# One kernel, one queue: SyncE's DMA instructions in program order through the whole attention stage

## The chip, the core and the metric

The kernel runs on one core of a Trainium2 chip. The metric is the device time of one execution in microseconds. In the profile TensorE is PE (its weight loads PEld), VectorE is DVE, ScalarE is ACT, GpSimd is POOL and SyncE is SP. SP computes nothing here: it is the queue from which most DMAs are issued, and its instructions appear as SPq. An instruction that has to wait holds up everything behind it on its own engine's queue. POOL issues DMAs too: the gathers and scatters by index, and the loads that convert their data on the way.

## What is computed

Block-causal attention over 8 batches and 8 heads, and on its rows a mixture of experts with one expert for each row:

```python
scores = scale * np.matmul(q, k.transpose(0, 1, 3, 2))          # q, k, v: (8, 8, 576, 64) float32
scores = np.where(block_i >= block_j, scores, -1e9)              # blocks of 64 positions
attn = softmax(scores); attn_out = np.matmul(attn, v)            # (8, 8, 576, 64)
x = attn_out.transpose(0, 2, 1, 3).reshape(8 * 576, 512)         # 4608 rows
logits = x @ w_gate + modality_bias[modality_id]                 # 8 experts
e_idx = argmax(logits); gate_w = softmax(logits)[e_idx]
out[rows of e] = gate_w * (relu(x[rows of e] @ w1[e]) @ w2[e])   # 512 -> 1024 -> 512
```

Everything is kept to float32 precision: PE's operands are split into a high and a low part, and each product is summed from several matmuls.

## The kernel before

**Attention** works on pairs of heads: 32 pairs, four pairs to a batch. A loop over slots (`run_slot`) works on pair `slot` and on pair `slot - 1` at once, by a list of steps written out by hand (`ORDER`; `FIRST` for slot 0, `LAST` for slot 32): scores S, maxima M, exponentials E, transposes T, their copies C and rests D, the products with v in the parts X, Y and W, the copies x and y, the product K with the gate's weights and an identity, and the rows Z. Before its steps a slot issues the loads of later pairs: `load(slot + 2)` (the tile `raw`, the keys), `load_v(slot + 1)` (`vrt`) and `split_qk(slot + 1)`. The last makes the high and low parts of the next pair on POOL and issues three kinds of DMA on SP: two copies `k2t<-z`, one copy `z<-qkt`, and the load `rawq` (queries) of the pair after. PE's first scores of a slot (L259, L260, step SA2) read that slot's `z`.

**Routing.** When the last pair of a batch b has its rows in the tile `xr` (and the 64 late positions in `xt`), `routing(b)` returns a list of some twenty small steps, which are taken one by one where `ORDER` has a q. One of them is `weight_out` (L503 to L514): two reciprocals on DVE (L504, L505), and then on SP the write of `xr` into the DRAM rows `xrows` (L507), two writes of `xt` (L511), the write of `wt` (L512) and a small load `idt` (L514), which the scatters into the expert lists will need. It falls near the end of slot 4b + 6, and for the last batches somewhat earlier.

**Into the experts.** During slots 30 to 32 the first expert's weights are loaded already (class `Experts`, `early`): `raw<-w` on SP (L809), a converted copy of each chunk on POOL (L813, called casts here), and the low part by a subtraction on POOL or DVE (L818). The row numbers of the first expert come by `ids_lead` (L831). Two gathers on POOL (L839, one for 128 rows) fetch 256 rows from `xrows` into `xr_124`, the tile that holds the rows of batch 6 until their write (L507) has read it. Their transposes (L852, step turn0) are PE's first work in slot 32, in front of the last pair's products (L383) and of the first expert product (L870). After attention `run_all` goes through parts of 256 rows, PE after PE product, to the end.

**What sets the order.** The kernel is written for a framework that orders instructions itself. Inside `manual_schedule(engines=...)` the named engines keep the order in which the program issues. PE, ACT, DVE and POOL are named all through. SP is named for the start and the first four slots:

Of the kernel before, what the change touches and what calls it, by code (L numbers as in the profile page):

```python
# [24 lines left out]
NPAIR = B * H // 2  # L25
# [11 lines left out]
LEAD = SLOT * NLEAD  # L37
BIG = float(1 << 20)
NWARM = 12
NSP = 4  # L40
SCALE = 0.125
GUARD = 1e-9
CHUNK_OFF = (0, 128, 384, 768)
# [49 lines left out]
def attention_moe(ctx, tc, qk, vr, bkw, mid, mb, w1, w2, cf, ci, cm, ld, out):  # L93
# [68 lines left out]
    def load(p):  # L162
        d = pairs[p]
        d.qk = qkts[p % 3]
        d.q = d.qk[:, 0:1280].rearrange("p (h c) -> p h c", h=2)
        d.k = d.qk[:, 1280:2432].rearrange("p (h c) -> p h c", h=2)
        d.qt = d.qk[:, 2432:2560]
        d.raw = raws[p % 2]
        d.q2, d.k2, d.pt = q2s[p % 2], k2s[p % 2], pts[p % 2]
        d.s, d.pm, d.copies, d.o, d.ot, d.b = {}, {}, {}, {}, {}, {}  # L170
        d.ott = None
        if p < 2:
            for h in range(2):
                ks, qs = halves(h)
                nc.sync.dma_start(d.raw[:, ks], qk[p][:, 1280:2560][:, ks])
                if p == 0:
                    nc.sync.dma_start(rawq[:, qs], qk[p][:, qs])
            pool.dma_start(zs[p][64:68], cm)
        else:
            nc.sync.dma_start(d.raw, qk[p][:, 1280:2560])  # L180
# [17 lines left out]
    def split_qk(p):  # L198
        d = pairs[p]
        k = d.raw[0:64, 0:1152].rearrange("p (h c) -> p h c", h=2)  # L200
        q = rawq[0:64].rearrange("p (h c) -> p h c", h=2)
        pool.tensor_copy(d.qk[:, 1280:2560], d.raw)
        pool.tensor_tensor(d.k2[0:64], k, d.k[0:64], ALU.subtract)  # L203
        gather_low(d)
        pool.tensor_copy(d.qk[:, 0:1280], rawq)
        nc.sync.dma_start(d.q2[0:64].bitcast(F32), d.q[64:128, :, 0:512].bitcast(F32))
        pool.tensor_tensor(d.q[0:64], q, d.q[0:64], ALU.subtract)  # L207
        load_q(p + 1)

    def split_half(p, h):  # L210
        d = pairs[p]
        ks, qs = halves(h)
        dve.tensor_copy(d.qk[:, 1280:2560][:, ks], d.raw[:, ks])
        act.copy(d.qk[:, qs], rawq[:, qs])
        (dve, pool)[p * h].tensor_tensor(d.k2[0:64, h], d.raw[0:64, 576 * h : 576 * h + 576], d.k[0:64, h], ALU.subtract)
        if h == 1:
            gather_low(d)
        act.copy(d.q2[0:64, h], rawq[0:64, qs][:, 0:512])
        (dve, pool)[p * h].tensor_tensor(d.q[0:64, h], rawq[0:64, qs], d.q[0:64, h], ALU.subtract)  # L219
        if (p, h) == (0, 1):  # L220
            load_q(1)
        if (p, h) == (1, 1):
            load(2)
            load_q(2)

    def load_v(p):
        d = pairs[p]
        d.vr = att.tile([128, 640], F32, name="vrt", bufs=3)
        nc.sync.dma_start(d.vr, vr[p])
        d.v = att.tile([128, 8, 2, 64], F32R, name="vhl", bufs=2)  # L230
# [337 lines left out]
    def choose(eng):  # L568
        lead, start = (cst.tile([128, NE], F32, name=n) for n in ("taken", "start"))
        eng.tensor_tensor(cnt, run, bases, ALU.subtract)  # L570
        sel["oha"], sel["ea"] = pick(eng, cnt, "a", kx, ranks)
        oha = sel["oha"]
        eng.scalar_tensor_tensor(cnb, oha, -BIG, cnt, ALU.mult, ALU.add)
        eng.scalar_tensor_tensor(lead, cnt, float(LEAD), oha, ALU.min, ALU.mult)
        sel["ohb"], sel["eb"] = pick(eng, cnb, "b", kx, ranks)
        eng.tensor_tensor(rest, lead, bases, ALU.add)
        sel["ra"] = dot(eng, oha, bases, "a")
        sel["rr"] = dot(eng, oha, rest, "r")
        sel["rb"] = dot(eng, sel["ohb"], bases, "b")
        eng.scalar_tensor_tensor(begin, oha, float(COVER - LEAD), rest, ALU.mult, ALU.add)  # L580
        eng.scalar_tensor_tensor(start, sel["ohb"], float(COVER_B), begin, ALU.mult, ALU.add)
        sel["start"] = start

    def emit(name, p):
        u = name[1:]
        if name == "vh":
            split_v(p)
        elif name == "r":
            sums(p)
        elif name == "p":  # L590
            inverses(p)
        elif name[0] == "S":
            scores(p, u)
        elif name[0] == "M":
            maxima(p, u)
        elif name[0] == "E":
            exps(p, u)
        elif name[0] == "T":
            transposes(p, u)
        elif name[0] == "C":  # L600
            copies(p, u)
        elif name[0] == "D":
            rests(p, u)
        elif name[0] in "XYW":
            values(p, "AB".index(u), name[0])
        elif name[0] in "xy":
            keep(p, "AB".index(u), name[0])
        elif name[0] == "K":
            back(p, "AB".index(u))
        elif name[0] == "Z":  # L610
            rows(p, "AB".index(u))

    done = set()
    lag = max(s for n, s in ORDER if n[0] != "q")
# [39 lines left out]
    def run_slot(slot):  # L654
        nonlocal steps, ex
        if 0 < slot < NPAIR - 2:
            load(slot + 2)
        if 0 < slot < NPAIR - 1:
            if slot > 1:
                load_v(slot + 1)  # L660
            split_qk(slot + 1)
        for name, stage in LAST if slot == NPAIR else ORDER if slot else FIRST:
            p = slot - stage
            for what in EARLY_STEPS.get((slot, name), ()):
                if ex is None:
                    ex = Experts(ctx, tc, cst, scratch, btmp, con["edges"], xrows, idlist, idf, w1, w2, out, sel, run, base8, pick, dot, ps_s, ps_t, ps_o, o0, placing, qkts, raws, zs, pts, xrb)
                ex.early(what)
            if name[0:6] == "+steps":
                for f in steps[0 : int(name[6:])]:
                    f()  # L670
                steps = steps[int(name[6:]) :]
                continue
            if name[0] == "+":
                ex.early(name[1:])
                continue
            if name[0] == "q":
                kind = "" if name[1].isdigit() else name
                for _ in range(2 if EARLY * PPB < slot < NPAIR - 1 and not kind else 1):
                    if slot > 1 and steps and getattr(steps[0], "kind", "") == kind:
                        steps.pop(0)()  # L680
                continue
            if not 0 <= p < NPAIR or (name, p) in done:
                continue
            assert slot < NPAIR or (name, 1) in ORDER
            if slot == 0:
                done.add((name, p))
                if name in first:
                    first[name]()
                    continue
            emit(name, p)  # L690
            if name == "vh":
                for _ in range(2):
                    if placing and slot < NPAIR:
                        g, c = placing.pop(0)
                        g(c)
            if name == "ZB" and p % PPB == PPB - 1:
                for f in steps:
                    f()
                steps = routing(p // PPB)
                if p // PPB == EARLY - 1:  # L700
                    choose(Later(dve, steps))

    engines = {ET.PE, ET.Activation, ET.DVE, ET.Pool}
    with tc.manual_schedule(engines=engines | {ET.SP}):
        load(0)
        for _ in range(NWARM):
            pe.matmul(bbank, ones, jks[0], start=True, stop=True)
        nc.sync.dma_start(cft, cf)
        split_half(0, 0)
        load(1)  # L710
        for slot in range(NSP):
            run_slot(slot)
    with tc.manual_schedule(engines=engines):
        for slot in range(NSP, NPAIR + lag):
            run_slot(slot)
        att_stack.close()
        ex.run_all(steps)
    ex.rest()
# [366 lines left out]
```

## Time and profile before

| | |
|---|---|
| median of 3 runs | 871.63 us (871.34 to 872.15) |
| the profiled execution | 871.13 us, of which the span from first to last instruction 869.5 us |
| mean granted TensorE clock | 0.983 |
| attention (slots 0 to 31) | up to about 408 us of the span |
| experts | from there to the end |

The rows that matter are quoted two sections down. In a timeline a row is one instruction or a run of like ones: its start, its duration, its engine and line, what it writes and reads, and in brackets how long its engine was idle before it and what ended that. For SP and POOL the duration of a DMA instruction is that of its issue; the data moves afterwards. A row of the windows gives for one stretch the busy time of each engine, PE's granted clock, the share of time in which the DMA engines were busy, and the rate.

### The profile page before, as it was taken

The page shows a single profiled execution, that of the slowest core. Times are in us where ns is not written, and L with a number is a line of the kernel's source. Part 1 is how long each engine was busy: PE and PEld are TensorE (multiplying, and loading weights), DVE is VectorE, ACT ScalarE, POOL GpSimd, SP SyncE. Part 2 cuts the span into 40 slices and gives each one's busy share as a digit, 9 for nine tenths or more (in the row PEclk, how much of TensorE's full clock was granted, in tenths as well). Part 3 has the DMA queues.
Part 4 walks back from the last instruction along what each step waited for, and adds up shares of the span by engine and source line. Part 5 has one row for each costly group of instructions (what it writes and reads, how often), then busy time and mean ns, then how long its engine had stood idle before and what let it go on. Part 6 is the DMA issues. An engine that isn't in the chain of part 4 may idle for free. (4 is left out here: it accounts for less than half of the span.)

```text
span 869.5 us, 16671 instructions
## 1 busy us (share of the span) xinstructions
PE 839.6 (97%) x5816; PEld 768.0 (88%) x5816; DVE 449.7 (52%) x1653; ACT 455.1 (52%) x1366; POOL 444.2 (51%) x300
## 2 busy tenths in 40 slices
PE   6999999999999999997999999999999999999995
PEld 4889999999999999897988999999999999999884
DVE  6798888888888888796442111111121122222120
ACT  6788888889888898786212222222222122222220
POOL 1967879798888979893864222222211111111100
PEclk8899999999999999999999999999999999999998
DMA  6869656766666667657752212212212222210100
GB/s 188 252 220 282 195 188 198 242 196 207 198 230 211 201 188 242 193 136 192 225 203 75 74 62 73 73 63 72 74 49 73 74 74 73 73 61 28 36 14 18
DMA packets 58183, 120.20 MB, mean 138 GB/s; under 512 B 13458, under 2 KB 24530, under 8 KB 58088
## 3 DMA queue, kind: packets, MB, share of 16 engines
q1 hardware_dynamic: 47344, 95.31, 35.7%
q0 software_dynamic: 10752, 23.79, 8.4%
q8 instruction: 48, 0.79, 0.4%
q14 instruction: 39, 0.32, 0.1%
HBM read 80.12 MB, written 22.25 MB: 118 GB/s over the span
## 5 line engine op out<-in xcount | busy, mean ns | idle before, releaser
L346 DVE TENSOR_TENSOR ptl<-t,pth 128x512 fp32r<-128x512 f32 (+3 forms) x288 | 139.9, 505 | 18.8 <-ACT pth L341 17.4
L341 ACT CAST pth<-t 128x512 fp32r<-128x512 f32 (+3 forms) x288 | 122.4, 452 | 36.2 <-PE t L316 22.8
L290 ACT ACTIVATE pm<-s,nm 128x256 f32<-128x256 f32 (+3 forms) x256 | 134.8, 535 | 11.3 <-DVE scratch L264 11.0
L264 DVE TENSOR_SCALAR_CACHE_REDUCE scratch<-s 128x128 bf16<-128x128 f32 (+4 forms) x288 | 133.0, 479 | 7.5 <-PE s L260 4.3
L383 PE MATMUL o<-pth,vhl 128*128 128x256 f32 (+1 forms) x384 | 116.2, 320 | 0.8 <-POOL vhl L236 0.6
L918 ACT ACTIVATE scratch<-o,gw 128x512 f32<-128x512 f32 x37 | 25.5, 689 | 173.0 <-PE o L916 102.0
L877 DVE SCALAR_TENSOR_TENSOR qkt<-s,qkt 128x512 fp32r<-128x512 f32 x18 | 12.4, 689 | 190.2 <-ACT qkt L876 190.2
L383 PE MATMUL o<-ptl,vhl 128*128 128x256 f32 (+1 forms) x384 | 109.3, 297 | 0.0
L203 POOL TENSOR_TENSOR z<-raw,qkt 64x1152 fp32r<-64x1152 f32 x30 | 79.5, 2650 | 47.7 <-issue 18.4
L919 POOL DMA_INDIRECT out<-scratch,ids_b x17 | 16.9, 996 | 162.7 <-ACT scratch L918 162.7
L259 PE MATMUL s<-qkt 128*128 128x256 f32 (+2 forms) x256 | 89.5, 360 | 3.7 <-DVE qkt L219 3.7
L870 PE MATMUL s<-z,w0hb 128*128 128x256 f32 x512 | 91.2, 281 | 0.0
L870 PE MATMUL s<-z,qkt 128*128 128x256 f32 x720 | 90.1, 283 | 0.6 <-issue 0.6
L870 PEld LDWEIGHTS s<-z,qkt 128*128 128x128 f32 x720 | 88.6, 192 | 1.3 <-issue 0.5
L207 POOL TENSOR_TENSOR qkt<-rawq,qkt 64x1280 fp32r<-64x1280 f32 x30 | 87.9, 2931 | 2.4
L260 PE MATMUL s<-z 68*128 68x256 f32 (+2 forms) x256 | 80.5, 330 | 0.0
L870 PEld LDWEIGHTS s<-z,w0hb 128*128 128x128 f32 x512 | 79.1, 188 | 0.6
L383 PEld LDWEIGHTS o<-pth,vhl 128*128 128x128 f32 x384 | 73.5, 191 | 3.1 <-POOL vhl L236 1.0
L383 PEld LDWEIGHTS o<-ptl,vhl 128*128 128x128 f32 x384 | 74.2, 193 | 1.4
L870 PE MATMUL s<-z,w0lb 128*128 128x256 f32 x256 | 71.9, 281 | 0.0
L402 PE MATMUL b<-bk,ot 128*128 128x72 f32 x512 | 64.7, 269 | 2.0 <-ACT pth L341 1.2
L402 PEld LDWEIGHTS b<-bk,ot 128*128 128x128 f32 x512 | 64.2, 192 | 2.4 <-ACT pth L341 1.4
(255 smaller groups left out, 1923.6 us busy)
## 6 DMA issues: line engine op xcount, KB each, us to landing
raw<-qk SPq DMA_DIRECT2D x30, 640.0 KB
rawq<-qk SPq DMA_DIRECT2D x30, 640.0 KB
raw<-w SPq DMA_DIRECT2D x23, 512.0 KB
vrt<-vr SPq DMA_DIRECT2D x32, 320.0 KB
k2t<-z SPq DMA_DIRECT2D x64, 144.0 KB
xrows<-xr SPq DMA_DIRECT2D x8, 1056.0 KB
z<-qkt SPq DMA_DIRECT2D x30, 256.0 KB
idlist<-btmp SPq DMA_DIRECT2D x8, 304.0 KB
```

Of the source, the lines that this page charges most:

```text
L203: pool.tensor_tensor(d.k2[0:64], k, d.k[0:64], ALU.subtract)
L207: pool.tensor_tensor(d.q[0:64], q, d.q[0:64], ALU.subtract)
L259: pe.matmul(o, d.q[:, h, qs], d.k[:, h, 0:n], start=True, stop=False)
L260: pe.matmul(o, d.q2[0:68, h, qs], d.k2[0:68, h, 0:n], start=False, stop=True)
L264: dve.tensor_scalar(jks[jturn[0] % 4][:, 0 : s.shape[-1]], s, -SCALE, start, ALU.mult, ALU.min, accum_out=o)
L290: act.activation(d.pm[h][:, CHUNK_OFF[c] : CHUNK_OFF[c] + n], s[:, 256 * i : 256 * i + n], AF.Exp, bias=d.nm[:, h, c : c + 1], scale=SCALE ...
L341: act.copy(dst[0], s)
L346: dve.tensor_tensor(dst[1], s, dst[0], ALU.subtract)
L383: pe.matmul(o, w, r, start=part != "W" and i == 0, stop=part != "Y" and i == len(mm) - 1)
L402: pe.matmul(d.b[h][:, 72 * c : 72 * c + 72], d.ot[h][:, 128 * c : 128 * c + 128], w, start=True, stop=True)
L870: nc.tensor.matmul(hp[:, a, :], w[:, kc, ms], x[:, kc, :], start=i == 0, stop=i == len(mm) - 1)
L918: nc.scalar.mul(yo, y, s.gw[:, i : i + 1])
```

## The change

The constant `NSP` goes, and the first of the two `manual_schedule` blocks, the one that names SP, takes all slots. The second block holds only what comes after attention.

```diff
-NSP = 4
...
         load(1)
-        for slot in range(NSP):
+        for slot in range(NPAIR + lag):
             run_slot(slot)
     with tc.manual_schedule(engines=engines):
-        for slot in range(NSP, NPAIR + lag):
-            run_slot(slot)
         att_stack.close()
         ex.run_all(steps)
```

Line numbers after the removed lines are lower by one to three (L507 becomes L506, L813 becomes L810). PE, DVE and ACT keep their instructions in the same order. The number of instructions is the same on every engine; SP's order changes, and POOL's in one place.

On SP around a batch's `weight_out`, here for batch 0 in slots 6 and 7, before. `z_111` takes the queries' second half of pair 7, `z_104` those of pair 8:

```order
L196 DMA k2t<-z_111 64x576 x2
L206 DMA z_111<-qkt_119 64x2x512
L188 DMA rawq<-qk 128x1280
L180 DMA raw_122<-qk 128x1280
L229 DMA vrt<-vr 128x640
L196 DMA k2t<-z_104 64x576 x2
L507 DMA xrows<-xr_124 128x4x528
L512 DMA xrows<-wt 64x16
L206 DMA z_104<-qkt_120 64x2x512
L188 DMA rawq<-qk 128x1280
```

And with the change:

```order
L195 DMA k2t<-z_111 64x576 x2
L205 DMA z_111<-qkt_119 64x2x512
L187 DMA rawq<-qk 128x1280
L506 DMA xrows<-xr_124 128x4x528
L510 DMA xrows<-xt 64x4x64 x2
L511 DMA xrows<-wt 64x16
L513 DMA idt<-ci 128x80
L179 DMA raw_122<-qk 128x1280
L228 DMA vrt<-vr 128x640
L195 DMA k2t<-z_104 64x576 x2
L205 DMA z_104<-qkt_120 64x2x512
L187 DMA rawq<-qk 128x1280
```

All five DMAs of `weight_out` now stand together between the load `rawq` of slot 6 and slot 7's loads; before, the two writes of `xt` went out a slot earlier, `idt` at some other time, and `xr` after the `k2t` copies of slot 7.

On SP in slot 30, before (`xr_124` holds batch 6, the `raw` loads are expert weights):

```order
L831 DMA ids_lead<-idlist 128x6x1
L809 ISA
L809 DMA raw_122<-w 128x4x256
L809 ISA
L809 DMA raw_121<-w 128x4x256
L507 DMA xrows<-xr_124 128x4x528
L512 DMA xrows<-wt 64x16
```

And with the change:

```order
L828 DMA ids_lead<-idlist 128x6x1
L506 DMA xrows<-xr_124 128x4x528
L510 DMA xrows<-xt 64x4x64 x2
L511 DMA xrows<-wt 64x16
L513 DMA idt<-ci 128x80
L806 ISA
L806 DMA raw_122<-w 128x4x256
L806 ISA
L806 DMA raw_121<-w 128x4x256
```

The write of `xr_124` moves ahead of two weight loads, the second of which waits for POOL's subtraction that frees `raw_121`.

On POOL in slot 32 and at the start of `run_all`, before:

```order
L818 TENSOR_TENSOR pth_105<-raw_121,pth_105 128x1024
L813 ISA
L813 DMA pth_112<-w 128x2x512
L818 TENSOR_TENSOR pth_112<-raw_122,ptl_106 128x1024
L818 TENSOR_TENSOR pth_112<-raw_121,pth_112 128x1024
L839 DMA xr_124<-xrows,ids_lead 128x528 x2
```

And with the change:

```order
L815 TENSOR_TENSOR pth_105<-raw_121,pth_105 128x1024
L836 DMA xr_124<-xrows,ids_lead 128x528 x2
L810 ISA
L810 DMA pth_112<-w 128x2x512
L815 TENSOR_TENSOR pth_112<-raw_122,ptl_106 128x1024
L815 TENSOR_TENSOR pth_112<-raw_121,pth_112 128x1024
```

The gather of the third part, which the second block issues, moves ahead of the first expert's last cast (`pth_112`) and of the two subtractions after it.

## Rows read from the trace of the kernel before

**Rows 1.** The page's busy times over the whole span: us, share, instructions.

```profile
PE 839.6 (97%) x5816; PEld 768.0 (88%) x5816; DVE 449.7 (52%) x1653; ACT 455.1 (52%) x1366; POOL 444.2 (51%) x300
```

**Rows 2.** What PE waited for over the whole span, the costliest: us in total, times, longest.

```profile
PE t L852 <- DMA xr<-xrows,ids_lead: 5.6, 2, 4.7
```

**Rows 3.** PE's timeline where attention ends and the experts begin.

```profile
412.49 0.45 PE L852 MATMUL t<-cf,xr 128*128 128x128 f32 x1 [4.67 <-DMA xr<-xrows,ids_lead]
413.88 0.90 PE L852 MATMUL t<-cf,xr 128*128 128x128 f32 x3 [0.94 <-DMA xr<-xrows,ids_lead]
...
418.30 3.03 PE L870 MATMUL s<-z,qkt 128*128 128x256 f32 x24
...
425.95 0.36 PE L383 MATMUL o<-pth,vhl 128*128 128x256 f32 x1
...
427.44 3.12 PE L870 MATMUL s<-z,z 128*128 128x256 f32 x24
...
434.87 0.60 PE L852 MATMUL t<-cf,xr 128*128 128x128 f32 x4
...
435.67 1.88 PE L916 MATMUL o<-pth,qkt 128*128 128x512 f32 x7
...
440.71 0.50 PE L916 MATMUL o<-pth,ptl 128*128 128x512 f32 x1 [0.39 <-POOL pth L818]
```

**Rows 4.** POOL's timeline of the same part.

```profile
397.87 0.76 POOL L813 DMA_DIRECT2D z<-w  x1
408.95 1.10 POOL L839 DMA_INDIRECT xr<-xrows,ids_lead  x1 [10.32 <-DMA xrows<-wt]
410.35 1.06 POOL L839 DMA_INDIRECT xr<-xrows,ids_lead  x1 [0.30 <-issue]
...
433.07 0.77 POOL L813 DMA_DIRECT2D pth<-w  x1
...
438.26 2.39 POOL L818 TENSOR_TENSOR pth<-raw,pth 128x1024 fp32r<-128x1024 f32 x1 [0.92 <-DMA pth<-w]
```

**Rows 5.** SP's timeline in slot 30.

```profile
388.89 0.66 SPq L831 DMA_DIRECT2D ids_lead<-idlist  x1
389.76 7.77 SPq L809 DMA_DIRECT2D raw<-w  x2
397.62 0.46 SPq L507 DMA_DIRECT2D xrows<-xr  x1
```

**Rows 6.** DVE's timeline at the reciprocals of `weight_out` that end the wait of the `xr` write: batch 6 (slot 30).

```profile
389.30 0.18 DVE L504 RECIPROCAL xr<-o 128x4 f32<-128x4 f32 x1
```

**Rows 7.** Windows where attention ends: the stretch, then busy time of PE, PEld, DVE, ACT and POOL, PE's granted clock, DMA share, GB/s.

```profile
400.00:408.00 8.00, 7.82 (x61) 7.09 (x59) 6.43 (x25) 7.17 (x26) 0.00 (x0) 1.00 0.98 280
412.40:415.00 2.60, 1.57 (x6) 1.31 (x7) 0.17 (x1) 0.18 (x1) 2.12 (x3) 0.50 0.26 84
415.00:418.00 3.00, 3.00 (x15) 2.68 (x15) 1.38 (x2) 1.36 (x3) 2.99 (x3) 0.62 0.02 5
```

**Rows 8.** DMA issues of the page: what moves, from which queue, how often, size of one.

```profile
raw<-qk SPq DMA_DIRECT2D x30, 640.0 KB
...
raw<-w SPq DMA_DIRECT2D x23, 512.0 KB
vrt<-vr SPq DMA_DIRECT2D x32, 320.0 KB
k2t<-z SPq DMA_DIRECT2D x64, 144.0 KB
xrows<-xr SPq DMA_DIRECT2D x8, 1056.0 KB
z<-qkt SPq DMA_DIRECT2D x30, 256.0 KB
...
qkt<-w POOLq DMA_DIRECT2D x3, 512.0 KB
...
xrows<-xt SPq DMA_DIRECT2D x16, 64.0 KB
...
idt<-ci SPq DMA_DIRECT2D x8, 40.0 KB
```

**Rows 9.** DVE's timeline at the reciprocal for batch 0 (slot 6).

```profile
99.84 0.17 DVE L504 RECIPROCAL xr<-o 128x4 f32<-128x4 f32 x1
```

**Rows 10.** SP's timeline in slots 6 and 7.

```profile
92.94 0.33 SPq L188 DMA_DIRECT2D rawq<-qk  x1
...
100.90 1.11 SPq L196 DMA_DIRECT2D k2t<-z  x2
...
103.34 1.32 SPq L206 DMA_DIRECT2D z<-qkt  x1
```

**Rows 11.** PE's timeline: the first read of pair 8's `z`, at the start of slot 8.

```profile
111.74 0.34 PE L260 MATMUL s<-z 68*128 68x384 f32 x1
```

**Rows 12.** Windows, columns as in rows 7: the stretch in which batch 0's `xr` becomes ready, the nine microseconds after its write is issued, a hundred microseconds of attention, and the experts.

```profile
99.00:102.00 3.00, 3.00 (x26) 2.95 (x25) 2.99 (x16) 2.79 (x10) 3.00 (x2) 1.00 0.02 5
102.00:111.00 9.00, 9.00 (x71) 8.29 (x70) 7.32 (x30) 7.78 (x28) 5.96 (x5) 1.00 1.00 324
100.00:200.00 100.00, 100.00 (x772) 93.83 (x770) 87.21 (x373) 88.29 (x306) 85.36 (x52) 1.00 0.65 203
460.00:840.00 380.00, 379.60 (x2431) 343.76 (x2430) 77.16 (x124) 91.69 (x146) 85.42 (x74) 1.00 0.20 64
```

## The prediction

> **What bounds the kernel now.** The page's busy times come first: PE works 839.6 us of a span of 869.5 [rows 1]. It takes its instructions in the order written, that order does not change, and no other engine is near; so the time falls only where PE stops waiting, and rises where it starts to. The list of PE's waits is short and has one large entry: 5.6 us for the first gather of expert rows [rows 2]. PE's timeline shows the place. PE is through with slot 31 at 412.49 - 4.67 = 407.82, the first transpose waits until 412.49, the next until 413.88, and the first expert product starts at 418.30 [rows 3]. The windows add a second cost of the same wait: PE's granted clock is at half, 1.2 GHz, between 412.4 and 415, and only by 418 back at 2.4 GHz [rows 7]. Next, POOL's timeline says why the gather is late: POOL stood idle 10.32 us, from the last of two casts at 398.63 to 408.95, for the writes into `xrows` [rows 4]. The gather's target is batch 6's `xr_124`, so it must wait until that tile is written out. SP's timeline says why the write is late: it is issued at 397.62, behind two weight loads that span 7.77 us [rows 5], although DVE's reciprocal, on which it depends, ran at 389.30 [rows 6]. So the order on SP costs PE time here. In the attention stage before, PE is busy 100.00 of 100 us [rows 12]: there the order on SP costs nothing now, and the question is whether the change makes it cost something.
>
> **The end of attention: the gain.** The write now stands right behind `ids_lead` and can issue at 389.6, 8.0 us earlier than 397.62 [rows 5, 6]. With it go two `xt` writes, `wt` and `idt`, ahead of the two weight loads; at about 0.6 us each they put the first load from 389.8 to about 393, and the second still waits for POOL's subtraction near 397, as it did. No other part of POOL's work before the gather changes, so the earliest gather is at 398.7, after the casts. Before, the write needed 408.95 - 397.62 = 11.3 us from issue to gather; the same 11.3 from 389.6 gives 400.9. The second gather follows 1.4 us later, and each needs 3.5 us to PE (408.95 to 412.49, 410.35 to 413.88 [rows 3, 4]): without anything in front, PE could go on at 403.6 to 405.8, before it wants to (407.82). That end is no wait at all.
>
> The other end: the gather's data comes through POOL's queue behind the two casts (512 KB each [rows 8]). From 400 to 408 the DMA engines moved 8 x 280 GB/s = 2.24 MB and were busy 0.98 of the time [rows 7]; of that the casts are 1.05 and the `xr` write 1.08. With the write gone from this stretch, and one weight load (0.52) and some 0.17 of small transfers moved into it, 1.85 MB remain: 6.6 us at the same rate, so the casts end near 406.6. The two gathers, 256 rows of 2112 bytes, are 0.54 MB, 1.9 us at that rate; with an estimated 0.5 us to the waiting engine PE gets the second at 409.0. Were the casts as late as the write was in the trace (408.4), it would be 411. I take 409.0, because the engines were full and a reorder removes no bytes.
>
> From the second gather PE has seven of eight transposes and the last pair's products before its first expert product. At full clock eight transposes take 435.67 - 434.87 = 0.80 and nine of the thirteen products 427.44 - 425.95 = 1.49 [rows 3], so 0.7 and about 2.1. The wait of 1.2 us in place of 5.6 I take to leave the clock up. With 0.2 us for the copies between, the product starts at 412.0 in place of 418.30: **6.3 us gained**. With no wait it is 407.8 + 0.8 + 2.1 = 410.7, 7.6 gained; with data at 411 and half clock for the same work (about 1.5 more) it is 415.4, 2.9 gained.
>
> On this transfer the Trainium skill speaks against the change (DMA: Bandwidth & Descriptors, "Issuing engines are not separate DMA queues"): DMAs of all issuers run on the same 16 DMA engines and interleave. A write moved ahead then competes with the casts earlier instead of later. The DMA share of 0.98 from 400 to 408 [rows 7] agrees that they were full there. By a sum that ignores it the gain would be 7.6, by one that takes it 6.3 or less.
>
> **The last cast: a small loss.** The gather of the third part now goes ahead of the cast of `pth_112` on POOL: two gathers of 1.06 to 1.10 us with 0.3 between [rows 4], 2.6 us, ahead of an instruction at 433.07 whose data POOL then subtracts at 438.26, and PE already waits 0.39 for that, at 440.71 [rows 3, 4]. But POOL's whole chain before it starts at the gather, now some 8 us earlier, while PE's need moves 6.3 earlier. So the wait grows by 2.6 + about 1 for the gather's own bytes in the queue - (8 - 6.3) = 1.9 at worst by this sum, and disappears if POOL was otherwise waiting; between -0.4 and 2.5 I take **0.4 lost**.
>
> **The batch ends: what queues behind the write.** In slots 4b + 6 the change adds a wait to SP. The write now follows `rawq` (92.94 for batch 0) but its data is ready only after the reciprocal at 99.84 + 0.17 [rows 9, 10]. SP stands some 6.8 us, and behind it the loads `raw` and `vrt`, the copies `k2t` and `z`, and the next `rawq`. The nearest need is PE's: pair 8's `z` at 111.74 [rows 11]. From 100.1 SP has to issue ten DMAs before the end of `z`, some 6 us, which is not the limit. The bytes are: 1056 + 128 + 4 + 40 + 640 + 320 + 288 + 256 = 2732 KB = 2.80 MB [rows 8]. The trace moves nearly the same mix right after this write at 324 GB/s [rows 12]: 8.6 us; started 1.2 us after issue (the `k2t` copies issued at 100.90 move almost nothing before 102 [rows 10, 12]), with an estimated 0.7 more for the 256-byte pieces of `xt` and 0.4 to land, `z` is there at 111.0. That is 0.7 us before the need, where today `z` is issued at 103.34 with time to spare. It happens for batches 0 to 4; for batch 5 the reciprocal and the queue's place coincide, and batch 6 is the case above. At 284 to 390 GB/s, the nearest rates about it, a stall lies between none and 0.5 us a batch; I take **0.7 us lost** in all five, range 0 to 4. `idt` and `xt` themselves cost nothing: the scatters that need `idt` come seven steps of the list later, and no gather reads `xrows` before slot 30.
>
> **The sum.** -6.3 + 0.4 + 0.7 = -5.2 us. After this part PE is busy 379.60 of 380 us [rows 12], so a gain ahead of it stays. The profiled execution, 871.13 us, would become 865.9; the median of the runs shown, 871.63, is 0.5 above it, so the forecast is 866.4, and its own ends are 864.0 (no wait for the gather and no loss, 7.6 gained) and 868.9 (6.3 gained, 1.1 lost at the cast and 2.5 at the batch ends).
>
> **Rivals.** (A) The gather stays late behind the casts: the bytes in front are the same and PE's queue starts up at half clock. For it speaks the DMA share near 1; against, that 1.08 MB leave this stretch. Gain 2.9 less the 1.1 of both losses: 869.8. It is where the Trainium skill's section named above leads if the interleaving takes all. (B) SP's new wait starves PE at the batch ends. If the 2.80 MB move at the attention's mean rate of 203 GB/s [rows 12] instead of 324, `z` is there at 101.3 + 13.8 + 0.4 = 115.5, 3.8 us late, and five batches cost 19 us: 871.6 - 5.9 + 19 = 884.7, slower. It decides from 1.2 us a batch (5.9 / 5), that is below about 250 GB/s. Against it: the mean is low because there are pauses, and with a full queue the trace shows 324. Half way (0.5 to 1.2 us a batch) the gain is eaten: 869 to 872. (C) The gain is given back at the last cast: if POOL's chain does not start earlier, PE waits 2.6 + 1 = 3.6 us more in place of 0.4: 866.4 + 3.2 = 869.6. (D) The order printed is not what costs: the gather waits for something else that I cannot see in the trace, and the time stays at 871.6.
>
> **Chances.** Forecast 0.64; A 0.10; B 0.18, of which slower 0.08, no change 0.08, still faster 0.02; C 0.06; D 0.02. About 0.2% (1.7 us) is what a measurement here can tell from no change: faster takes the forecast, some 0.09 of A and C, whose times lie about that bound, and the 0.02 of B, 0.75; same the other 0.07 of A and C, 0.08 of B and D, 0.17; slower 0.08. The range 863.7 to 870.3 holds the forecast with its ends, A, C and the faster part of B; it leaves out D, the slower part of B and most of its middle, and a gain above 7.9, together under 0.2.
>
> **What would show it.** The write of batch 6 is issued near 389.7 and the gather near 399 to 401; POOL's 10.32 us idle shrink to under 3; PE's wait for the gather falls from 5.6 to about 1 and the half-clock stretch there goes. PE has no new wait at L260 at the starts of slots 8, 12, 16, 20 and 24, while SP's own list shows a new wait on DVE at the `xr` write, some 7 us five times. PE's wait for `pth` stays below 1 us. I am wrong if PE waits for `z` at batch ends, if the gather's data reaches PE after 411, or if the wait for `pth` exceeds 2.

## The result, and the profile after

The changed kernel takes 880.1 us in the median (877.91 to 882.03), the kernel before 871.89 (871.34 to 872.66) beside it: ratio 1.0093, 95% interval 1.0067 to 1.0118. It is slower; 866.4 had been forecast, with a range up to 870.3. The profiled execution took 877.91 us (span 876.3).

PE's and SP's waits of the changed kernel: what waits, for what; us in total, times, longest.

```profile
PE s L259 <- DMA z<-qkt: 8.5, 5, 3.1
...
PE o L913 <- POOL pth L815: 1.0, 1, 1.0
...
SPq L506 <- DVE wt L504: 35.5, 7, 6.8
```

PE's wait of 5.6 us for the first gather [rows 2] is gone from the list, and a wait of 8.5 us for `z`, in five pieces, has come. SP's new wait at the rows' write is the one that was foreseen, up to 6.8 us.

PE's timeline at the starts of slots 8, 12, 16, 20 and 24, the first reads of the new `z` (in brackets the idle time before):

```profile
113.90 0.44 PE L259 MATMUL s<-z 68*128 68x384 f32 x1 [1.50 <-DMA z<-qkt]
...
163.57 0.44 PE L259 MATMUL s<-z 68*128 68x384 f32 x1 [0.58 <-DMA z<-qkt]
...
214.04 0.44 PE L259 MATMUL s<-z 68*128 68x384 f32 x1 [1.37 <-DMA z<-qkt]
...
265.00 0.45 PE L259 MATMUL s<-z 68*128 68x384 f32 x1 [1.88 <-DMA z<-qkt]
...
317.20 0.44 PE L259 MATMUL s<-z 68*128 68x384 f32 x1 [3.11 <-DMA z<-qkt]
```

The first of these stood at 111.74 in the kernel before [rows 11], the last at 307.07: PE is 2.2 us behind after the first batch end and 10.1 after the fifth. Of this, 0.5 us is older than the first batch end. It shows in the matmul just ahead of the first of these reads, in the kernel before and in the changed one:

```profile
111.48 0.42 PE L259 MATMUL s<-qkt 128*128 128x384 f32 x1
```

```profile
111.98 0.42 PE L258 MATMUL s<-qkt 128*128 128x384 f32 x1
```

PE has it from 44.6 us on, for the most part from a wait for DVE there, 0.75 us in place of 0.42.

Windows behind the fifth stall (us; busy time of PE, PEld, DVE, ACT, POOL with instructions; granted clock, DMA share, GB/s):

```profile
318.00:320.00 2.00, 2.00 (x14) 2.00 (x12) 1.54 (x9) 1.40 (x6) 1.31 (x2) 0.61 0.93 279
320.00:322.00 2.00, 2.00 (x11) 1.55 (x10) 1.26 (x6) 0.82 (x5) 2.00 (x1) 0.54 0.52 129
```

After that stall the clock is at its lower level, 1.2 GHz, for most of 4 us (0.61 and 0.54 of full), which costs another (0.39 + 0.46) x 2 = 1.7 us. PE's lag behind the kernel before agrees: it grows from 10.1 to 11.7 us there.

SP's timeline at the first batch end (start, time to issue):

```profile
93.44 0.33 SPq L187 DMA_DIRECT2D rawq<-qk  x1
100.53 0.38 SPq L506 DMA_DIRECT2D xrows<-xr  x1
100.97 2.08 SPq L510 DMA_DIRECT2D xrows<-xt  x2
103.14 0.99 SPq L511 DMA_DIRECT2D xrows<-wt  x1
104.17 0.58 SPq L513 DMA_DIRECT2D idt<-ci  x1
104.80 0.43 SPq L179 DMA_DIRECT2D raw<-qk  x1
...
105.80 1.14 SPq L195 DMA_DIRECT2D k2t<-z  x2
107.04 0.62 SPq L205 DMA_DIRECT2D z<-qkt  x1
107.75 1.04 SPq L187 DMA_DIRECT2D rawq<-qk  x1
108.84 0.73 SPq L179 DMA_DIRECT2D raw<-qk  x1
```

The copy into `z` is issued at 107.04, where the kernel before issued it at 103.34 [rows 10], and reaches PE 6.9 us later. Just behind it come `rawq` and `raw` for later pairs, 1280 KB. Windows of the changed kernel over the same stretch (columns as above):

```profile
101.40:112.80 11.40, 10.99 (x85) 9.99 (x83) 9.69 (x41) 10.17 (x37) 8.42 (x5) 1.00 0.97 268
...
101.40:104.60 3.20, 3.20 (x24) 2.88 (x23) 2.74 (x17) 2.75 (x10) 3.12 (x2) 1.00 0.98 349
104.80:107.20 2.40, 2.40 (x24) 2.40 (x23) 1.96 (x8) 2.36 (x10) 2.01 (x2) 1.00 0.86 137
107.20:108.80 1.60, 1.60 (x12) 1.25 (x11) 1.60 (x6) 1.53 (x6) 0.00 (x0) 1.00 0.92 360
108.80:112.80 4.00, 3.59 (x30) 3.32 (x30) 3.19 (x13) 3.33 (x12) 3.09 (x2) 1.00 1.06 251
```

The rate falls twice: to 137 GB/s when the rows are through, and to 251 where the copies `k2t` and `z` move and the loads behind them begin, with the DMA engines full (1.06). The first fall is not at the time when SP issues the small pieces (100.97 to 104.75), for then the rows still move at 349. It is when these pieces themselves move, from 104.28 to 105.98 by the DMA packets that the trace recorded; the first packet of `raw`, which SP issued only behind them, starts at 105.85.

The end of attention, SP, POOL and PE of the changed kernel, from their timelines:

```profile
401.12 0.57 SPq L506 DMA_DIRECT2D xrows<-xr  x1
```

```profile
410.97 0.75 POOL L810 DMA_DIRECT2D z<-w  x1
412.02 1.09 POOL L836 DMA_INDIRECT xr<-xrows,ids_lead  x1 [0.30 <-DVE rc L358]
```

```profile
418.97 0.27 PE L329 MATMUL t<-cf,pm 128*128 128x128 f32 x1
419.08 0.93 PE L849 MATMUL t<-cf,xr 128*128 128x128 f32 x4
...
422.31 0.28 PE L867 MATMUL s<-z,qkt 128*128 128x256 f32 x1
423.73 0.74 PE L867 MATMUL s<-z,qkt 128*128 128x256 f32 x4 [1.13 <-DVE z L853]
...
446.73 0.50 PE L913 MATMUL o<-pth,ptl 128*128 128x512 f32 x1 [0.98 <-POOL pth L815]
```

POOL's 10.32 us of idleness ahead of the gather [rows 4] have become 0.30, and the transposes follow attention with no wait, where PE had waited 4.67 us and more [rows 3]. PE is 11.4 us behind the kernel before when attention ends (419.24 against 407.82), of which 10.9 came at the batch ends. It is 5.3 behind from the second expert product on (423.73; in the kernel before the products run from 418.30 [rows 3], the second at 418.42), and 6.0 behind at the product that reads `pth` (446.73 against 440.71). So the end gave back 6.1 us, the last cast took 0.6, and the batch ends had taken 10.9.

### The profile page after: what moved, and what is told of

The parts are those of the page before. It is cut to its first block, busy times and chain, and to the rows that moved or that the text cites. A ratio compares the mean times of both kernels' runs of the same rounds, so it can differ in the third digit from the quotient of the medians.

```text
span 876.3 us, 16656 instructions
## 1 busy us (share of the span) xinstructions
PE 841.0 (96%) x5816; PEld 767.8 (88%) x5816; DVE 453.2 (52%) x1653; ACT 454.8 (52%) x1366; POOL 444.5 (51%) x300
## 5 line engine op out<-in xcount | busy, mean ns | idle before, releaser
L289 ACT ACTIVATE pm<-s,nm 128x256 f32<-128x256 f32 (+3 forms) x256 | 134.4, 534 | 11.4 <-DVE scratch L263 10.9
```

What stands on the lines that cost most here:

```text
L289: act.activation(d.pm[h][:, CHUNK_OFF[c] : CHUNK_OFF[c] + n], s[:, 256 * i : 256 * i + n], AF.Exp, bias=d.nm[:, h, c : c + 1], scale=SCALE ...
```

## The experiments

The theory after the result: the gain at the end and the loss at the batch ends are two separate things, and the loss is `z` coming late because of what the change puts between the wait's end and `z`. What of it counts was open: SP's time for the small DMAs, the bytes of the rows, the wait alone, or more. Each kernel was timed beside the kernel before, and every ratio below is to that. Line numbers shift with the lines that a run adds.

**Program order at the end only.** The manual blocks are split:

```diff
-        for slot in range(NPAIR + lag):
+        for slot in range(4):
+            run_slot(slot)
+    with tc.manual_schedule(engines=engines):
+        for slot in range(4, 28):
+            run_slot(slot)
+    with tc.manual_schedule(engines=engines | {ET.SP}):
+        for slot in range(28, NPAIR + lag):
             run_slot(slot)
```

> SP in program order in slots 0 to 3 and from slot 28 on only; the scheduler orders SP in slots 4 to 27. Theory (the loss sits in five batch ends, the gain at the end of attention): the stalls at the starts of slots 8, 12, 16, 20 and 24 go (PE there fell 11.4 us behind the kernel before) and the end keeps its 6.1 us less what the last cast and the run-up cost (some 1.3): about 867 us, between 866 and 868.5. Rival (the place of the stalls is a symptom of something that the end's order brings): the time stays above 873.

Measured: 866.08 us, ratio 0.9940 (0.9926 to 0.9953), 5.7 us faster. PE does not wait for `z` at all. PE's timeline at the end of attention of this kernel:

```profile
408.07 0.30 PE L855 MATMUL t<-cf,xr 128*128 128x128 f32 x1
408.63 0.55 PE L855 MATMUL t<-cf,xr 128*128 128x128 f32 x3 [0.26 <-DMA xr<-xrows,ids_lead]
...
411.49 2.79 PE L873 MATMUL s<-z,qkt 128*128 128x256 f32 x22
```

The first expert product starts at 411.49; the prediction had said 412.0, against 418.30 [rows 3]. The gain is what the prediction took it for, and it needs nothing from the batch ends.

**Program order at the batch ends only.** The complement: SP in program order in slots 0 to 27.

```diff
-        for slot in range(NPAIR + lag):
+        for slot in range(28):
             run_slot(slot)
     with tc.manual_schedule(engines=engines):
+        for slot in range(28, NPAIR + lag):
+            run_slot(slot)
```

> The complement of the run with program order at the end only: SP in program order in slots 0 to 27, the scheduler's order from slot 28 on. Theory (two separate effects that add): the stalls of the batch ends stay and the gain at the end is not there, 871.8 plus the 14.0 that lie between the changed kernel and the order at the end only, 884 to 886 us; from the profiles, 871.1 + 11 to 12, 882.5. So 882 to 886. Rival (the stalls are partly made up at the end of attention, since the late PE finds the gather ready): the wait for the first gather shrinks by what PE is late, so that only some 5 us remain, 875 to 878 us.

Measured: 890.31 us, ratio 1.0205 (1.0177 to 1.0232), slower than either expectation. PE's waits of this kernel:

```profile
PE s L259 <- DMA z<-qkt: 10.0, 5, 2.4
...
PE t L851 <- DMA xr<-xrows,ids_lead: 6.2, 2, 5.3
```

The wait for the gather is no shorter than before (6.2 us against 5.6), though PE comes to it 18 us later: nothing is made up at the end, since SP and POOL are late with PE. The stalls sum to 10.0 us, but half clock follows four of the five. Windows of 4.8 to 5 us from each stall's end:

```profile
115.00:120.00 5.00, 5.00 (x29) 4.55 (x28) 3.12 (x15) 2.48 (x9) 3.83 (x2) 0.66 0.92 285
167.20:172.00 4.80, 4.80 (x26) 4.54 (x26) 2.95 (x13) 2.22 (x8) 2.88 (x2) 0.66 0.79 259
219.70:224.50 4.80, 4.80 (x35) 4.41 (x36) 3.84 (x21) 2.95 (x11) 3.30 (x2) 1.00 0.87 278
271.00:276.00 5.00, 4.82 (x26) 4.38 (x27) 3.04 (x15) 2.23 (x8) 3.40 (x2) 0.68 0.95 307
323.60:328.60 5.00, 4.96 (x26) 4.70 (x27) 3.11 (x15) 2.23 (x8) 3.46 (x2) 0.66 0.85 284
```

That is 0.34 x 4.8 = 1.6 us more, or a little above, for each of four, some 6.6 in all. The two halves do not add to the whole (-5.7 and +18.2 against +8.2): in the changed kernel's profile only one stall of five brought the half clock. Why the same order brings it more often here stays open.

**All five output DMAs behind z.** A list holds the DMAs of a batch until the next slot's `split_qk` has issued its copy into `z`:

```diff
+            held.append(write) if b < 5 else write()
+            held.append(small) if b < 5 else small()
...
         pool.tensor_tensor(d.q[0:64], q, d.q[0:64], ALU.subtract)
+        while held:
+            held.pop(0)()
         load_q(p + 1)
```

(`write` is the rows' write, `small` the two `xt`, `wt` and `idt`.)

> SP in program order throughout, but for batches 0 to 4 the five output DMAs of a batch (rows, two xt, wt, idt) stand behind the next slot's copy into z, ahead of the next rawq. Both theories of what makes z late (the four small DMAs, or the bytes of the rows) expect z's copy at about 103 us as in the kernel before, no wait of PE for z, and 867 us (866 to 868.5). Rival (the loads behind the write, rawq above all, are what is late, and PE only shows it at z): the stalls move one slot on and over 3 us of the loss stay, 870 or more.

Measured: 865.40 us, ratio 0.9927 (0.9913 to 0.9942), no wait for `z`, and `rawq` coming later does not show on PE. A second time:

> The kernel with the five output DMAs behind z once more, beside the one before it: 865.4 us within 0.5.

Measured: 866.00 us, 0.9939 (0.9921 to 0.9956).

**One part of the five behind z.** Three kernels leave part of the DMAs in the changed kernel's place. First the small ones behind, the rows in place:

```diff
+            write()
+            held.append(small) if b < 5 else small()
```

> The rows' write stays in its place with its wait, and the four small DMAs (two xt, wt, idt: 3.8 us of SP) stand behind the next copy into z. Theory 1 (the small DMAs make z late: SP is 3.8 us in issuing them and the DMA engines move some 115 GB/s meanwhile): raw can start as the rows end, at 104.6, raw and vrt take 2.5 us at 390 GB/s, k2t and z 2.4 us at 230, z is there near 110.5 against a need at 112.4; stalls vanish but for some 0.3 us in the last, 867 to 868.5 us. Theory 2 (the 1.08 MB of the rows make it late, the DMA engines being full): 2.63 MB at the 246 GB/s of the changed kernel take 10.7 us from 101.45, z is there at 113.2, the stalls shrink by 0.7 each: 875 us.

Then the rows behind, the small ones in place with `wt` first, so that the wait stays where it was:

```diff
+            held.append(write) if b < 5 else write()
+            small()
```

> The reverse: wt (with the wait), two xt and idt stay in front, and the rows' write of 1.08 MB stands behind the next copy into z, for batches 0 to 4. Theory 1 (SP's time for the small DMAs): z's copy is still issued 6.5 us after the wait ends, starts some 2.7 us later and lands near 112.5; 0.1 to 0.8 us of stall a batch stay and more in the last: 869 to 873 us. Theory 2 (bytes): with 1.08 MB out of the way z is there 2.8 us earlier or more, all stalls but the last vanish: 867 to 868 us.

Then only `wt`, 4 KB, in place:

```diff
+            queue.dma_start(xrows[S * b + 512 : S * b + S, 512:XW], g.wt[64:128])
+            held.append(write) if b < 5 else write()
+            held.append(small) if b < 5 else small()
```

> Program order throughout; for batches 0 to 4 only wt (4 KB), which waits for the same reciprocal, stays in the changed kernel's place; the rows' write, the two xt and idt stand behind the next copy into z. Theory (the wait is harmless in itself, what counts is all that is put between the wait and z): z's copy is issued near 103.5, 1.5 MB at 250 GB/s from 102.2 put z at 109.4 against 112.4, no wait of PE, 865 to 867 us. Rival (the stop of the queue alone is enough, since raw, vrt and all behind them start 6 us late and POOL then runs late): over 2 us of the stalls stay, 868 or more.

Measured: small behind 867.94 (ratio 0.9955, 0.9938 to 0.9973), with PE's waits for `z` down to 1.6 us in four; rows behind 866.33 (0.9938, 0.9925 to 0.9951), none; `wt` alone 865.49 (0.9927, 0.9912 to 0.9943), none. Theory 1 forecast the first and missed the second; theory 2 missed the first, and of the second it had the stalls right and the time 0.7 us too high. Neither the small DMAs nor the rows are the cause alone, either one out of the way brings `z` back under PE's need, or within 0.5 us of it. And the wait is harmless by itself: with `wt` alone SP still stands until 100.58 (from 93.68), as its timeline shows, and then has `z`'s copy out at 103.46, as early as before [rows 10]:

```profile
93.35 0.33 SPq L188 DMA_DIRECT2D rawq<-qk  x1
100.58 0.47 SPq L521 DMA_DIRECT2D xrows<-wt  x1
...
103.46 0.62 SPq L206 DMA_DIRECT2D z<-qkt  x1
```

**The five DMAs between k2t and z.**

```diff
         gather_low(d)
+        while held:
+            held.pop(0)()
         pool.tensor_copy(d.qk[:, 0:1280], rawq)
```

> For batches 0 to 4 the five output DMAs stand behind the k2t copies and ahead of the copy into z, so that raw and vrt go out before the wait. Theory of bytes: between the wait's end and z stand k2t, the rows, the small ones and z, 1.8 MB, at 250 GB/s z is there at 110.8 against 112.4, no stall, 865 to 867.5 us. Theory of SP's issue time: z's copy is issued at 106.7 as in the changed kernel and needs the 5.9 to 8.4 us from issue to PE that it needed there, so 112.6 to 115.1: stalls of 0.3 to 2.7 a batch stay, 872 to 877 us.

Measured: 866.15 us (0.9929, 0.9916 to 0.9942), no wait of PE for `z`. With `raw` and `vrt` (0.98 MB) sent before the wait, the rows and small DMAs may all stand ahead of `z`. Its copy is issued at 107.69, later than in the changed kernel, and `rawq` and `raw` follow at 108.40 and 109.00; yet PE reads `z` at 112.59 without a wait. The theory of SP's issue time falls.

**k2t behind z, in every slot.**

```diff
-        gather_low(d)
         pool.tensor_copy(d.qk[:, 0:1280], rawq)
         nc.sync.dma_start(d.q2[0:64].bitcast(F32), d.q[64:128, :, 0:512].bitcast(F32))
+        gather_low(d)
```

> The changed kernel with the order of the two copies exchanged in every slot: z first, then k2t (295 KB less in front of z, and z's copy issued 1.2 us earlier). Theory of bytes: 295 KB at 230 to 250 GB/s are 1.2 to 1.3 us less of each of the five stalls (1.7, 0.9, 1.6, 2.1, 3.4), 5.8 us in all: 873 to 875 us against 880.1. Theory that the small copies run beside the other transfers and their place does not count: 879 to 881. If PE now waits for k2t in place of z, the wait is at another line and the time as before the exchange or longer.

Measured: 869.78 us (0.9976, 0.9964 to 0.9989), some 10 us less than the changed kernel's 880.1, more than the 6 of the theory of bytes; PE's list has 1.6 us in two waits for `z` left. The place of 295 KB counts; the surplus was open then.

**The small DMAs ahead of the rows, in place.** SP can issue them while it would stand still:

```diff
-            queue.dma_start(xrows[S * b : S * b + 512, :].rearrange("(c p) w -> p c w", p=128), xr)
             late = xrows[S * b + 512 : S * b + S, :]
...
                 queue.dma_start(cols[:, :, a, :], xt[64 * a : 64 * a + 64, :, 8:72])
-            queue.dma_start(late[:, 512:XW], g.wt[64:128])
             g.idt = t([128, 5, IW], I32, name="idt")
             queue.dma_start(g.idt, ci[b].rearrange("p (c w) -> p c w", c=5))
+            queue.dma_start(xrows[S * b : S * b + 512, :].rearrange("(c p) w -> p c w", p=128), xr)
+            queue.dma_start(late[:, 512:XW], g.wt[64:128])
```

> Program order throughout, all five output DMAs at the changed kernel's place, but within it the two xt and idt stand ahead of the rows' write. Their data is there before the reciprocal, so SP issues them while it would stand still, and only the rows and wt come between the wait's end and raw. Theory (what counts is all that stands between the wait's end and z, in SP's time and in bytes): about as with the small DMAs behind z, stalls of 0 to 0.6 a batch, 866 to 868.5 us. Rival (the place in the program is what costs, in whatever order within it): 875 or more.

Measured: 873.12 us (1.0014, 0.9997 to 1.0030). Both expectations missed. SP and PE at the first batch end:

```profile
105.27 0.62 SPq L205 DMA_DIRECT2D z<-qkt  x1
105.98 0.88 SPq L187 DMA_DIRECT2D rawq<-qk  x1
106.92 1.20 SPq L179 DMA_DIRECT2D raw<-qk  x1
```

```profile
114.15 0.44 PE L259 MATMUL s<-z 68*128 68x384 f32 x1 [1.67 <-DMA z<-qkt]
```

The copy is issued 1.8 us earlier than in the changed kernel (107.04), and `z` comes no earlier (114.15 against 113.90). With the small DMAs behind `z` PE waited 0.5 at this place. There the copy was issued 0.3 us earlier (104.97), and PE came to it 0.4 later (112.86 against 112.48), which is some 0.7 of the difference of 1.2. What else differs is behind `z`: here `rawq` and `raw` follow at once, there they come 5 us later.

**The loads behind z held back.** `idt` is loaded twice more behind `z`, each load waiting for the last, ahead of the next `rawq`; nothing in front of `z` changes. Once in the changed kernel, once in the kernel just shown:

```diff
             queue.dma_start(g.idt, ci[b].rearrange("p (c w) -> p c w", c=5))
+            if b < 5:
+                for _ in range(2):
+                    held.append(lambda: queue.dma_start(g.idt, ci[b].rearrange("p (c w) -> p c w", c=5)))
```

> The changed kernel, but at the ends of batches 0 to 4 idt is loaded twice more behind z's copy, each load waiting for the one before, so that the next rawq and raw (1.28 MB) leave SP some 3 us later (near 111 in place of 107.75) and reach the DMA engines after z has passed; what stands in front of z is unchanged. Theory (the loads behind z share the DMA engines with it: z's packets take 3.1 to 4.8 us where the loads start beside them): z's packets are through up to 1 us earlier, the stalls shrink by 0.5 to 1 each and the half clock behind them goes, 871 to 875 us. Rival (only what stands in front of z counts): 878 to 880.

> The kernel with the small DMAs ahead of the rows' write in place (873.1 us, stalls of 1.1 to 1.8), and the same two further loads of idt behind z's copy, so that rawq and raw come some 3 us later. Theory (the loads behind z share the engines with it; this is why the small DMAs behind z gave 867.9 and the small DMAs ahead of the rows 873.1, with z's copy issued at the same place): the stalls shrink to 0.6 or less, 867 to 869 us. Rival (only what stands in front of z counts): 872 to 874.

Measured: 873.89 us (1.0014, 1.0000 to 1.0027) in place of 880.1, and 866.73 (0.9933, 0.9921 to 0.9946) in place of 873.12: about 6 us each. In the first, PE still waits for `z` 5.4 us in four, the longest 2.0, with no half clock behind: the loads behind `z` are a part of the changed kernel's loss, and another part is left in what stands in front. SP and PE of the second at the first batch end:

```profile
105.32 0.62 SPq L206 DMA_DIRECT2D z<-qkt  x1
105.99 6.68 SPq L517 DMA_DIRECT2D idt<-ci  x2
112.76 0.38 SPq L188 DMA_DIRECT2D rawq<-qk  x1
```

```profile
112.36 0.34 PE L262 MATMUL s<-z 68*128 68x384 f32 x1
```

The copy is issued at 105.32 as in its twin, and PE reads `z` at 112.36 without a wait. From 108 to 113 the two kernels' windows read, the twin without the hold first:

```profile
108.00:113.00 5.00, 4.48 (x36) 3.95 (x35) 4.18 (x15) 4.25 (x16) 3.21 (x2) 1.00 1.05 235
```

```profile
108.00:113.00 5.00, 5.00 (x42) 4.73 (x41) 4.18 (x15) 4.26 (x17) 3.17 (x2) 1.00 0.57 124
```

The DMA engines were full (1.05) with `z` and the loads behind it together, and `z` paid for that: by the recorded packets its last one ends at 112.88 there, and at 111.63 with the loads held back. What is issued after a copy can take part of the engines from it. It did not where less stood in front: with the five DMAs between `k2t` and `z` the same loads followed and PE did not wait. The loads behind may also be the surplus of the run with `k2t` behind `z`, where `k2t` stands between `z` and those loads; no run separates it.

**The last cast, and the changed kernel again.** One kernel with the five DMAs behind `z` has slots 32 and 33 in the block of the expert stage, so that POOL keeps the old order of the last cast:

```diff
-        for slot in range(NPAIR + lag):
+        for slot in range(NPAIR):
             run_slot(slot)
     with tc.manual_schedule(engines=engines):
+        for slot in range(NPAIR, NPAIR + lag):
+            run_slot(slot)
```

> The kernel with the five output DMAs behind z, and slots 32 and 33 in one block with the expert stage as in the kernel before, so that POOL casts pth_112 ahead of the third part's gathers again. Theory (the gathers ahead of the cast cost PE's wait for pth, 1.7 us in that kernel's profile against 0.4 before): 1 to 1.3 us less than the same kernel without it, 864 to 864.5 against 865.4. Rival (POOL is no earlier, since the cast waits for something else): no difference.

Measured: 865.29 us (0.9919, 0.9904 to 0.9934) beside the 866.00 of its twin; the intervals overlap, so the theory is neither shown nor refuted. PE's wait for POOL's `pth` is gone, and 0.59 us for DVE's `pth` stand in its place.

> The changed kernel once more, for the spread of its runs: they went from 877.9 to 882.0, where the kernel before stays within 1.3. Theory (a stall of PE at a batch end costs its own length, and in some executions half clock behind it): the profile shows PE's waits for z of 8 to 11 us in five, half clock behind some of them and not others, and a slower run has more of it; 878 to 883 us. Rival (the spread comes from elsewhere): the waits and the clock behind them are as in the first profile while the time differs.

Measured: 878.39 us (1.0079, 1.0064 to 1.0093), runs from 878.35 to 879.73. PE waits 9.3 us for `z` in five, the longest 2.6, and half clock follows only the last. The spread of the first set was not met again, so its cause stays unsettled.

## Why the prediction was wrong

**The end of attention: right.** Predicted 6.3 us, measured 6.1 in the changed kernel. In the run with program order at the end only, the first expert product came at 411.49 for a predicted 412.0. The gather was issued right behind the casts, as the sum had it. Two small terms were off and cancelled in the changed kernel: no wait for the gather (1.2 expected), but 1.13 us for DVE's copy of the transposed rows (0.2 expected). Rival A did not come, though the DMA engines were full (a share of 1.26 from 412 to 415 in the changed kernel). No row shows the 0.5 us that the sum had from the gather's data to PE; PE waited 0.26 at most there in these two kernels.

**The last cast: right.** Predicted 0.4, measured 0.6. (The two gathers are 2.5 us by [rows 4], not 2.6.) Rival C did not come.

**The batch ends: the step that failed.** The prediction had the place, the wait and the queue behind it right: SP's wait at the rows' write of some 7 us, `z`'s copy out 6.5 us after it (some 6 expected), and a need 11.9 us after the reciprocal. It priced the way to `z` as 2.80 MB at 324 GB/s and got 0.7 us in all; the batch ends took 10.9. The 324 came from the right stretch of the other kernel [rows 12], but from another order. Here the rate was 349 for the rows, 137 while the small pieces moved and `raw` began, and 251 for the copies. Over 101.4 to 112.8 that is 268 GB/s, 3.06 MB; of these some 0.26 MB were no part of the 2.80, by the difference, and may be the loads issued behind `z`, the first packet of which starts at 110.98 beside it. The prediction's sum stopped at `z`, as if the queue were served in order; the runs that held those loads back show that they were worth some 6 us of the 14 that lie, in the medians, between the changed kernel and the run with program order at the end only.

A second term of the same sum was too small: 0.4 us to land. No row of the kernel before gave it, nor the 0.7 for the pieces of `xt`, nor the 284 and 390 GB/s of the range. The recorded packets of the changed kernel show the landing: the last packet of `z` ends at 112.83, 1.06 us before PE's read, and 0.90 to 1.06 before it at all five batch ends. At the first, `z` came 1.7 us after PE's need where the sum had it 0.7 before. Of these 2.4 us the bytes are 2.1 (11.4 from the rows' first packet at 101.45, in place of 8.6 + 0.7) and the landing 0.7, less 0.3 for an earlier start.

The Trainium skill has a rule that bears on this, beside the one that the prediction had weighed for the gather (DMA: Bandwidth & Descriptors, "Two DMAs through the same engine are not ordered"): within one queue of one DMA engine descriptors start in order but are pipelined, and nothing orders DMAs across the 16 engines. This case agrees: with the same issue time `z` came at 114.15 with the loads behind it and by 112.36 without.

**A term that was missing.** The price of a stall was its own length. Of the 10.9 us, PE's waits for `z` are 8.5 in the list, and the half clock behind the last some 1.6; the rest lies in the restarts behind the waits. In the kernel with program order at the batch ends only, some 6.6 us are half clock. The prediction knew the half clock as part of the gain at the gather [rows 7] and did not charge it on the other side.

**The sum.** -6.1 + 0.6 + 10.9, with the 0.5 from before the batch ends, is +5.9; the profiled executions differ by 877.91 - 871.13 = 6.8. PE's lag is 6.0 us at 446.73 and 6.5 from 464 to its last product, and 0.3 more lies behind that; neither was followed to a cause.

**Rivals and chances.** Rival B happened, and in its mechanism: SP's wait and a rate too low for the bytes in front of `z`. It named 250 GB/s as the rate below which the gain is lost, and the 2.80 MB took 11.4 us, 246 GB/s. What made the rate low it did not have. It took PE's need and 203 GB/s for a stall of 3.8 us; the stalls were 0.6 to 3.1. It had a chance of 0.18, and of ending slower 0.08, which was too little: the forecast left 0.7 us of room on a rate that no row gave for this mix, and 2.80 MB at 284 to 390 was too narrow a range for it.

## What to carry to other kernels

A DMA's arrival depends on what is issued before it and on what follows at once; a sum of the bytes ahead, at a rate from another order, left out 2.4 us here at the first batch end, three times its margin. When an instruction that must wait is put ahead of loads, the wait may cost nothing and the pile-up behind it everything: look for a place for the bulky and the small writes behind the copy that the busiest engine needs next, which here turned 880.1 us into 865.4, faster than the kernel before too. Charge a stall of the matrix engine with the half clock that may follow it.

## What the runs showed of the hardware

- DMAs issued by one queue, one after the other, are not served strictly in that order: holding back 1280 KB issued behind a 256 KB copy brought the copy to PE at least 1.8 us earlier (by 112.36, where PE did not wait, against 114.15) with its issue at the same place (105.32 and 105.27).
- A copy's packets spread out when much is queued around it. The 128 packets of `z` start within 1.3 us in the kernel before, and with the five DMAs between `k2t` and `z` within 1.3 to 2.1; in the changed kernel it takes 2.0 to 4.2. From the end of the last one to PE's read are another 0.9 to 1.1 us there.
- The half clock after a stall is not a matter of the stall's length alone: it followed stalls of 1.67 us (small DMAs ahead of the rows, clock 0.66 in the 5 us behind it) and 1.83 (batch ends only), and did not follow one of 1.97 in that same run, nor 1.88 in the changed kernel, nor 2.28 in its second profile. What decides, no run here shows.
- The two small strided writes of `xt`, 64 KB each, took SP 2.08 us to issue where the write of 1056 KB took 0.38, and in the window in which the small pieces moved and `raw` began, the DMA engines were 0.86 busy at 137 GB/s.
